# Quarter-array keys and scores, a half-plain first product for batch 1, a snapshot sum on VectorE, and a new written order

## The chip, the cores and the metric

The kernel runs on one core of a Trainium2 chip. The metric is the device time of one execution in microseconds (us). The core has five engines that run side by side and meet at semaphores: TensorE (PE in the profile, with its weight loads as a row of their own, PEld), VectorE (DVE), ScalarE (ACT), GpSimd (POOL) and SyncE (SP). Transfers are issued from the queues of POOL and SP here.

## The reference, cut to what matters

Four batches, 8 heads, 768 tokens, 64 values per head. `P` is an 8x8 matrix per batch and head (five rounds of row and column normalisation of `sort_net`).

```
k_sorted[i] = sum_j P[i, j] k_block[j]        (8 blocks of 96 tokens; v the same)
attn        = softmax(q_block k_sorted_block^T / 8) v_sorted_block
x           = heads side by side, [4, 768, 512]
u           = x + real(fft over tokens of fft over features of x)
un          = (u - mean) / sqrt(var + 1e-6)
out         = u + relu(un @ w_ch1) @ w_ch2    (512 -> 2048 -> 512)
```

So each batch has a stage of attention, a stage of Fourier mixing and a stage of two matrix products, called here the first and the second MLP product.

## The kernel before

**Attention** (`kqt`, `scores`, `av`) takes two heads at a time, a pair. A key step (line 1117) multiplies the loaded keys (128 partitions, six tokens in each) by a mask `bdk` that holds `P` of the head, so that the block sum and the transposition are one product; per pair it is 12 matmuls, in two groups of six, each on 128 rows by 64 columns of the array with 128 moving columns. The queries of batches 0 and 1 are transposed by TensorE (line 1148, 12 per pair); those of batches 2 and 3 by DMA. A score step (line 1176) is eight matmuls on 64 rows by 128 columns, 96 moving columns each, and there are two such steps per pair. ScalarE takes the exponential (line 1185), VectorE or ScalarE subtract one (1198, 1200), and `av` (1215) multiplies by the values.

**Fourier mixing** (`dft1`, `dft2`) is products with tables (lines 1299 to 1394) and sums on VectorE (1259 to 1343, 1403, 1417).

**The MLP.** Batch 0 is plain: `ff1` (line 1539) makes 32 steps of four matmuls with 384 moving columns, a relu out of PSUM follows each (1548 on VectorE, 1551 on ScalarE), and the second product is line 1597. Batches 1 to 3 use a form of matrix multiplication with seven block products in place of eight, over the two token halves and two halves of the weights. In the first product (`ff1_seven`, `pair`) a pair of blocks of 128 hidden features takes 14 matmuls (line 1680) in place of 16; running sums in PSUM are copied out by ScalarE (a snapshot, line 1705), VectorE adds them to another bank (1688) and takes the relu (1699); one of the four results has its relu straight out of PSUM on ScalarE (1722). `SEVEN[b]` says which of the eight pairs of a batch take this form; those ahead of it are plain. It needs sums of weights (`w1_sums`, 1639, two halves of four sums) and of inputs (1668). In the second product (`ff2_chunk`, line 1792) each chunk of 128 tokens takes seven products of eight matmuls (p1 to p7). There ScalarE copies two running sums into one tile of 512 columns (1817), and a DMA with addition issued by POOL (1835) adds that tile to `u`, which VectorE's last add (1812) then reads and adds the product to. The results are stored by SP (1561 to 1570) and, for rows that come out reversed, by POOL (1574).

**What sets the order.** All work is registered as numbered steps (`P.add`), with what each reads and writes. `ORDER` is a written list of step numbers for each engine; `Plan.schedule` replays it with estimated durations to choose the buffers. The numbers count the calls of `P.add`, so adding a step shifts all later ones. `MODE`, `TRIM` and `FETCH` only serve these estimates. Early on, TensorE is fed with idle matmuls (line 1951) until the first Fourier stage of batch 0 is done.

## Time and profile before

| | |
|---|---|
| median of 3 runs | 258.97 us (258.86 to 259.05) |
| the profiled execution | 259.09 us, its span 257.3 us |
| granted TensorE clock, mean | 0.997 |
| busy: PE / PEld / DVE / ACT / POOL | 244.6 / 166.5 / 229.7 / 177.5 / 63.0 us |
| instructions | 6768, of them 2596 matmuls and as many weight loads |

The span is from the first to the last instruction; the 1.8 us beside it are the start and the end of the execution, which the profile does not show. A matmul's row is longer than its turn: a new one starts while the last one drains, so the turn is read from the distance of starts, not from the mean duration. An add that waits for several things is put down to the one that came last.

### The profile page before, as it was taken

How to read it: one execution, taken by the hardware profiler on the slowest of the kernel's cores; microseconds unless marked ns; L12 is line 12 of the kernel's file. 1: busy time of each engine (PE TensorE's matmuls, PEld its weight loads, DVE VectorE, ACT ScalarE, POOL GpSimd, SP SyncE). 2: the span in 40 equal slices, each digit the busy share in tenths (PEclk: the TensorE clock that was granted, in tenths of full speed). 3: DMA queues.
4: the chain of work that ended last, by engine and by line, in shares of the span. 5: the costliest groups of instructions: out<-in, count | busy, mean ns of one | idle time of the engine just before them, and what ended most of it. 6: DMA issues, size and time to landing. Idle time of an engine off the chain costs nothing.

```text
span 257.3 us, 6768 instructions
## 1 busy us (share of the span) xinstructions
PE 244.6 (95%) x2596; PEld 166.5 (65%) x2596; DVE 229.7 (89%) x616; ACT 177.5 (69%) x410; POOL 63.0 (24%) x90
## 2 busy tenths in 40 slices
PE   4799999999999999999999999999999999999990
PEld 1346775576765756655665558887567887568880
DVE  4799999999999999999999999969999976999651
ACT  2599999989879999999828875437985315772110
POOL 8985123323200480000005001322000113001560
PEclk9999999999999999999999999999999999999998
DMA  7999999999980599555605303872221533000496
GB/s 136 201 222 300 221 208 216 206 245 189 166 107 3 95 193 194 132 124 98 199 9 161 132 1 85 176 199 44 82 23 23 102 64 82 3 0 0 103 254 217
DMA packets 46566, 33.53 MB, mean 130 GB/s; under 512 B 30554, under 2 KB 39528, under 8 KB 46532
## 3 DMA queue, kind: packets, MB, share of 16 engines
q0 software_dynamic: 24832, 20.67, 47.5%
q1 hardware_dynamic: 21702, 12.43, 20.8%
q8 instruction: 20, 0.33, 0.5%
q14 instruction: 12, 0.10, 0.2%
HBM read 31.39 MB, written 8.65 MB: 156 GB/s over the span
## 4 chain that ended last, share of the span: by engine, by line
PE 79%; DVE 13%; DMA 3%; ACT 2%; issue 1%; DVEq 0%; ACTq 0%
PE bank L1680 21%; PE bank L1792 20%; PE bank L1597 8%; PE bank L1539 7%; PE bank L1215 4%; PE bank L1176 2%; PE bank L948 2%; DMA u<-vsf 2%; PE bank L1299 2%; PE bank L1390 2%; PE bank L1117 2%; DVE rt L1234 2%; PE bank L1049 1%; PE bank L1394 1%; DVE eb L1198 1%
## 5 line engine op out<-in xcount | busy, mean ns | idle before, releaser
L1705 ACT COPY vsf<-bank 128x384 f32<-128x384 f32 x63 | 28.3, 481 | 12.2 <-PE bank L1680 11.3
L1688 DVE TENSOR_TENSOR hr<-bank,vsf 128x384 f16<-128x384 f32 x63 | 32.7, 549 | 0.9 <-PE bank L1680 0.4
L1680 PE MATMUL bank<-ut,w1sb 128*128 128x384 f16 x144 | 31.6, 326 | 0.0
L1792 PEld LDWEIGHTS <-hr 128*128 128x128 f16 x288 | 28.0, 98 | 5.2 <-issue 0.9
L1185 ACT ACTIVATE ex<-bank 96x384 f32<-96x384 f32 x64 | 29.0, 486 | 1.2 <-PE bank L1176 0.6
L1680 PEld LDWEIGHTS <-w1sb 128*128 128x128 f16 x192 | 18.7, 98 | 11.7 <-issue 0.2
L1817 ACT COPY vsf<-bank 128x256 f32<-128x256 f32 x18 | 6.7, 372 | 26.2 <-PE bank L1792 23.1
L1597 PE MATMUL bank<-w2sb,hr 128*128 128x512 f16 x96 | 24.7, 379 | 0.0
L1539 PE MATMUL bank<-ut,w1sb 128*128 128x384 f16 x128 | 24.7, 327 | 0.0
L1792 PEld LDWEIGHTS <-kq 128*128 128x128 f16 x216 | 21.1, 98 | 2.9
L1574 POOL DMA_INDIRECT out_dram<-u,rows x9 | 9.5, 1050 | 52.8 <-DVE u L1604 41.0
L1680 PEld LDWEIGHTS <-vcx 128*128 128x128 f16 x144 | 14.1, 98 | 9.2
L1812 DVE TENSOR_TENSOR u<-bank,u 128x256 f32<-128x256 f32 (+1 forms) x25 | 11.3, 471 | 8.9 <-PE bank L1792 5.1
L626 POOL DMA_DIRECT2D kq<-in_q_dram x18 | 15.1, 854 | 12.3 <-DMA w2sb<-in_moe_w_ch_dram 5.9
L1215 PEld LDWEIGHTS <-eb 97*128 97x128 f16 x416 | 15.6, 98 | 3.7 <-issue 0.7
L1792 PE MATMUL bank<-w2sb,hr 128*128 128x256 f16 x144 | 17.9, 273 | 0.0
L1792 PE MATMUL bank<-kq 128*128 128x256 f16 x144 | 17.8, 273 | 0.0
L1835 POOL DMA_DIRECT2D u<-vsf x6 | 5.4, 894 | 49.2 <-ACT vsf L1817 49.2
L1200 ACT ACTIVATE eb<-ex,negone 96x384 f16<-96x384 f32 x28 | 17.3, 616 | 0.1
L1215 PE MATMUL bank<-vsf,eb 97*128 97x65 f16 x416 | 17.0, 193 | 0.3 <-DVE vsf L842 0.2
L1234 DVE TENSOR_TENSOR rt<-bank,rz 128x384 f16<-128x384 f32 x32 | 16.9, 545 | 0.2
L1539 PEld LDWEIGHTS <-w1sb 128*128 128x128 f16 x128 | 11.1, 98 | 7.2 <-issue 0.3
(200 smaller groups left out, 593.1 us busy)
## 6 DMA issues: line engine op xcount, KB each, us to landing
kq<-in_k_dram POOLq DMA_DIRECT2D x6, 384.0 KB, 11.9
spilled<-u SPq DMA_DIRECT2D x9, 256.0 KB
u<-spilled SPq DMA_DIRECT2D x9, 256.0 KB, 4.4
w1sb<-in_moe_w_ch_dram POOLq DMA_DIRECT2D x4, 512.0 KB, 19.9
w2sb<-in_moe_w_ch_dram POOLq DMA_DIRECT2D x4, 512.0 KB, 20.3
hr<-in_v_dram POOLq DMA_DIRECT2D x2, 768.0 KB, 9.0
kq<-in_v_dram POOLq DMA_DIRECT2D x2, 768.0 KB, 15.6
kq<-in_q_dram POOLq DMA_DIRECT2D x16, 96.0 KB, 7.2
```

Source lines behind the costliest of these rows:

```text
L626: o = P.add({eng: c}, lambda _: e.dma_start(dst, src), r=r, w=w, prio=prio, nbytes=nbytes, tag="load", after=after)
L1185: nc.scalar.activation(ex.ap[0:96], pss[h2].ap[0:96, 0:384], AF.Exp, scale=SCALE),
L1200: nc.scalar.activation(ed, src, AF.Identity, bias=negone[0:96])
L1215: nc.tensor.matmul(po.ap[:, 65 * T:65 * T + 65], eb.ap[:, e0:e0 + 128], vsf[0:97, vi:vi + 65], start=(n == 0), stop=(n == len(WIN[T]) - 1) ...
L1234: V.tensor_tensor(rt.ap[:, :, D * h:D * h + D], po3()[:, :, 0:D], rz.ap[:, :, None].broadcast_to([128, 6, D]), op=ALU.mult)
L1539: nc.tensor.matmul(ps.ap[:, 0:GT], w1sb[:, c, 128 * fc:128 * fc + 128], ut.ap[:, c, :], start=(c == 0), stop=(c == 3))
L1597: nc.tensor.matmul(ps.ap, hr[g][:, fc, 128 * tt:128 * tt + 128], w2sb[:, fc, :], start=(fc == 0), stop=(fc == 15))
L1680: nc.tensor.matmul(ps.ap[:, 0:GT], lhs[:, c, fi], rhs()[:, c, :], start=(start and c == 0), stop=(c == 1), skip_group_check=True)
L1688: return P.add({"DVE": (0.47, 0.57)}, lambda _: V.tensor_tensor(hr[g][:, fc, :], p.ap[:, 0:GT], flat(o).bitcast(F32), op=ALU.add), r=r, w= ...
L1705: P.add({"ACT": act(GT)}, lambda _: nc.scalar.copy(flat(x).bitcast(F32), A.ap[:, 0:GT]), r=[A], w=[x], prio=pr_v - 1, tag="pc")
L1792: nc.tensor.matmul(ps.ap[:, o:o + 256], lhs()[:, fc], rhs[:, fc], start=(start and fc == 0), stop=(fc == 7), skip_group_check=True)
L1812: P.add({"DVE": (c, c + 0.1)}, lambda _: V.tensor_tensor(u.ap[:, lo:lo + n], p.ap[:, o:o + n], u.ap[:, lo:lo + n], op=ALU.add), r=r, w=w, ...
```

## The change

Five edits:

1. `SEVEN[1]` is (4, 8) in place of (0, 8): the first four of the eight pairs of batch 1 take the plain form of 16 matmuls, with four relus out of PSUM each. The first half of `w1_sums` is then made ahead of batch 2.
2. `QUAD`: for batches 1 to 3 the key step is 24 matmuls on 64 rows by 64 columns with 64 moving columns, four after each other on the four quarters of the array; the two row halves go to two PSUM banks, and one evacuation of 384 columns follows each. The tokens lie otherwise for it: each half of the keys is loaded by two DMAs of 64 partitions, which wait for all earlier users of the place (`gone`). The mask has eight columns per block in place of 16, from a permuted copy of `P` (`make_tk8`: one more matmul, one evacuation and one small load). The score step is 16 matmuls on quarters, still 96 moving columns. The queries of batch 1 are transposed by 24 matmuls on quarters and evacuated in two halves.
3. In the very last chunk VectorE adds the snapshot tile to `u` (`xadd`), in place of the DMA with addition.
4. `FLEX`: the relu of the seven-product form, and a subtraction in the value path, may also stand on ScalarE.
5. All five lists are new. TensorE has 494 steps before and 471 after, ScalarE 398 and 414, VectorE 604 and 570, POOL 74 and 80, SP 79 and 79.

In TensorE's list, the steps of keys, transposes and scores of batches 1 to 3 have these numbers. Before: keys 332, 348, 364, 380 (and each plus 2), 588, 603, 618, 633 (plus 2), 683, 698, 713, 728 (plus 2); transposes 336, 352, 368, 384; scores 338, 354, 370, 386, 593, 608, 623, 638, 688, 703, 718, 733 (and each plus 5). After: keys 337, 353, 369, 385, 595, 609, 623, 637, 688, 702, 716, 730; transposes 340, 356, 372, 388; scores 343, 359, 375, 391, 599, 613, 627, 641, 692, 706, 720, 734 (and each plus 5). The last chunk is, after: p6 1599, xadd 1601, p7 1602 (its add 1603), p4 1604 (1605), p2 1607 (1608, store 1609), p3 1610 (1611, store 1612); 1588, 1585 are p4 and p3 of the chunk before it (add 1586).

```diff
-SEVEN = {0: (8, 8), 1: (0, 8), 2: (0, 8), 3: (0, 8)}
+SEVEN = {0: (8, 8), 1: (4, 8), 2: (0, 8), 3: (0, 8)}
-FLEX = ()
+FLEX = ("relu", "vcd")
 ORDER = { "PE": (
...
-        "205 325 332 348 334 350 352 315 327 321 244 248 250 257 255 338 384 "
-        "259 263 267 343 284 289 430 364 368 366 431 294 275 432 278 281 396 "
-        "354 854 359 1648 380 870 399 564 868 382 860 402 405 386 856 304 571 "
-        "848 850 572 846 852 308 391 370 864 858 375 872 417 414 312 844 411 "
-        "842 408 603 588 605 590 862 449 874 866 497 501 465 886 503 447 875 "
-        "463 876 475 459 877 593 473 887 598 608 618 888 461 445 613 508 889 "
-        "455 510 620 633 457 471 467 469 453 451 512 516 520 880 648 537 881 "
-        "657 542 882 892 623 635 883 651 628 902 912 906 654 894 638 910 908 "
-        "900 643 698 683 918 547 914 896 660 700 685 922 663 904 898 666 916 "
-        "703 669 920 927 688 928 708 693 929 713 728 930 730 715 743 933 777 "
-        "746 934 718 752 749 781 979 978 783 723 733 935 738 788 755 939 764 "
...
-        "1603 1615 1600 1618 1630 1620 1634 1623 1637 1639 1645 1642 "
+        "325 331 356 340 323 329 319 246 250 252 257 259 337 261 265 269 343 "
+        "435 291 296 436 437 277 286 280 283 353 348 865 359 1613 843 853 401 "
+        "369 364 857 404 845 571 873 410 863 407 578 851 306 450 859 579 388 "
+        "385 867 847 372 861 310 871 391 375 855 849 380 396 869 881 464 452 "
+        "882 875 609 595 462 883 416 413 314 422 419 884 468 470 876 478 480 "
+        "877 599 466 903 613 604 878 456 895 476 887 454 637 618 911 460 458 "
+        "888 474 504 623 905 472 901 651 917 654 657 508 889 641 660 890 921 "
+        "627 646 893 515 897 909 517 510 669 899 923 688 632 519 907 523 527 "
+        "913 544 549 663 934 666 716 915 672 935 919 936 720 692 937 928 554 "
+        "725 697 940 929 941 702 730 942 778 744 930 756 931 782 706 759 747 "
+        "784 791 964 734 711 962 952 739 753 789 750 956 762 990 765 954 1007 "
...
+        "1578 1563 1575 1568 1580 1565 1583 1595 1597 1599 1588 1602 1585 "
+        "1604 1610 1607 "
...
     "DVE": (
...
+        "1584 1593 1566 1569 1589 1598 1603 1586 1605 1601 1611 1608 "
...
+QUAD = (1, 2, 3)
...
+        if nm == "k" and b in QUAD:
...
+            for n in range(2):
+                load(qk16(nm, b, hf).rearrange("p h r d -> p h (r d)")[
+                    64 * n:64 * n + 64],
+                    src[b, 4 * hf:4 * hf + 4].rearrange(
+                        "h (w e r) d -> e w h (r d)", e=2, r=6)[n],
+                    393216, keys[2 * n:2 * n + 2], prio, after=after,
+                    gone=gone)
...
+    def make_tk8():
+        load_c("perm", 29.0)
+        pt = Buf("pf")
+        flat = tkh.rearrange("p i b -> p (i b)")
+        P.add(pe(0.12, 1), lambda _: nc.tensor.matmul(
+            pt.ap[:, 0:256], perm[:, 0:128], flat), r=["perm", "tkh"],
+            w=[pt], tag="tk8")
+        P.add(evac(256), lambda e: copy(e, flat, pt.ap[:, 0:256]),
+              r=[pt], w=["tkh"], tag="tk8e")
...
+    def q_four(b, hp):
...
+            for r in range(6):
+                for n in range(2):
+                    for h2 in range(2):
+                        c = slice(64 * n, 64 * n + 64)
+                        nc.tensor.matmul(
+                            pts[n].ap.bitcast(F16)[
+                                64 * h2:64 * h2 + 64, 64 * r:64 * r + 64],
+                            q16[c, 2 * hl + h2, r, :], idh[c, c],
+                            is_transpose=True)
...
+    def kq_four(b, hp, k16, ks):
...
+            for r in range(6):
+                for n in range(2):
+                    for h2 in range(2):
+                        c = slice(64 * n, 64 * n + 64)
+                        nc.tensor.matmul(
+                            pss[n].ap[64 * h2:64 * h2 + 64,
+                                      64 * r:64 * r + 64],
+                            k16[c, 2 * hl + h2, r, :],
+                            bdk8[c, 2 * hp + h2].rearrange("p i c -> p (i c)"))
...
     def scores(b, hp):
...
-                    for h2 in range(2):
-                        rows = slice(64 * h2, 64 * h2 + 64)
-                        nc.tensor.matmul(
-                            pss[h2].ap[:, BLK * j:BLK * j + BLK],
-                            ks.ap[rows, 4 * g + j, :],
-                            qt.ap[rows, c0:c0 + BLK])
+                    for n in range(2 if four else 1):
+                        for h2 in range(2):
+                            c = slice(64 * n, 64 * n + (64 if four else 128))
+                            rows = slice(64 * h2, 64 * h2 + 64)
+                            nc.tensor.matmul(
+                                pss[h2].ap[c, BLK * j:BLK * j + BLK],
+                                ks.ap[rows, 4 * g + j, c],
+                                qt.ap[rows, c0:c0 + BLK])
...
+            if final:
+                P.add({"DVE": (0.6, 0.69)}, lambda _: V.tensor_tensor(
+                    u0.ap, u0.ap, x_(0, 512), op=ALU.add),
+                    r=[(X, 0), (X, 1), u0], w=[(u0, "x")], prio=pr_v,
+                    tag="xadd")
+                return
             P.add({"POOL": (1.0, 4.0)}, lambda _: nc.gpsimd.dma_start(
                 u0.ap, x_(0, 512), accum_op=ALU.add),
                 r=[(X, 0), (X, 1), u0], w=[(u0, "x")], prio=pr_v, tag="xacc")
```

More of the change, by code (lines that the diff above doesn't have):

```diff
@@ L621, with load @@
     w2v = moe_w_ch2.rearrange("(c p) m -> p c m", p=128)
-    def load(dst, src, nbytes, w, prio, eng="POOL", r=(), after=()):
+    def load(dst, src, nbytes, w, prio, eng="POOL", r=(), after=(), gone=()):
         e = {"POOL": nc.gpsimd, "SP": nc.sync}[eng]
@@ L626, in load @@
         o = P.add({eng: c}, lambda _: e.dma_start(dst, src), r=r, w=w,
-                  prio=prio, nbytes=nbytes, tag="load", after=after)
+                  prio=prio, nbytes=nbytes, tag="load",
+                  after=list(after) + list(gone))
         o.late = 6.0 if after else 0.0
@@ L675, in load_qk @@
                     after=after)
+            return
+        if nm == "k" and b in QUAD:
+            keys = kqk(slot[nm, b, hf])
+            gone = set()
+            for x in keys:
+                gone.update(P.wr.get(x, ()))
+                gone.update(P.rd.get(x, ()))
+            for n in range(2):
[5 more added lines that the diff above has]
+                    gone=gone)
             return
```

112 lines of the change are left out of this document (84 added, 28 removed), and 187 rows, old and new, of the table ORDER.

## The prediction

> **What bounds the kernel now.** I read the page's sums first, then the chain that ended last, then the busy time by stage, then single instructions at the end and around the key and score steps.
>
> ```profile
> PE 244.6 (95%) x2596; PEld 166.5 (65%) x2596; DVE 229.7 (89%) x616; ACT 177.5 (69%) x410; POOL 63.0 (24%) x90
> ...
> PE 79%; DVE 13%; DMA 3%; ACT 2%; issue 1%; DVEq 0%; ACTq 0%
> ```
>
> TensorE carries 79% of the chain, VectorE 13%. A mean hides that these lie in different stages. The pieces of the chain (start, length, what):
>
> ```profile
> 49.66 0.91 DVE un L1484 x2
> ...
> 58.53 0.76 PE bank L1539 x4
> ...
> 136.84 15.47 PE bank L1680 x94
> ...
> 155.36 10.48 PE bank L1792 x96
> ...
> 233.00 13.11 PE bank L1792 x120
> 246.13 0.38 ACT vsf L1817
> 246.81 5.89 DMA u<-vsf
> 252.79 0.42 DVE u L1812
> ```
>
> And the busy time by stage (first column the stretch, then PE, PEld, DVE, ACT, POOL, granted clock, DMA share, GB/s):
>
> ```profile
> 33.00:57.00 24.00, 23.72 (x365) 15.88 (x365) 23.45 (x72) 22.43 (x55) 7.20 (x10) 1.00 1.15 216
> 98.00:122.00 24.00, 24.00 (x313) 14.37 (x312) 22.98 (x58) 23.08 (x58) 0.00 (x0) 1.00 0.71 136
> 137.00:170.00 33.00, 33.00 (x248) 23.76 (x246) 30.82 (x90) 22.08 (x53) 5.55 (x8) 1.00 0.49 123
> 246.00:257.30 11.30, 4.62 (x41) 3.74 (x39) 2.60 (x7) 0.37 (x1) 3.46 (x6) 0.92 0.77 239
> ```
>
> Three parts are to be seen. Up to about 58 us the chain is on VectorE, with ScalarE full beside it (23.45 and 22.43 of 24 us). From 58.53 to 246 it is TensorE, without a gap: 94 matmuls of 384 columns in 15.47 us are 0.165 us each, 120 of 256 columns in 13.11 us are 0.109, so 0.43 ns a column, the same in both. Then comes an end of 11 us in which TensorE works for 4.62. There the chain is the accumulating DMA, 5.89 us. So three things pay: less turn time on TensorE after 58 us, less in that end, and less VectorE and ScalarE work ahead of 58 us.
>
> **The end: the snapshot sum on VectorE.** The last instructions in order of time (start, length),
>
> ```profile
> 246.81 1.04 PE L1792 MATMUL bank<-tab,hr 128*128 128x256 f16 x8
> 247.88 0.76 DVE L1812 TENSOR_TENSOR u<-bank,u 128x256 f32<-128x256 f32 x2 [1.21 <-PE bank L1792]
> 248.36 1.03 PE L1792 MATMUL bank<-kq,hr 128*128 128x256 f16 x8 [0.52 <-DVE u L1812]
> 249.23 1.04 PE L1792 MATMUL bank<-w2sb,kq 128*128 128x256 f16 x8
> 250.10 1.04 PE L1792 MATMUL bank<-w2sb,hr 128*128 128x256 f16 x8
> ...
> 250.23 0.96 POOL L1574 DMA_INDIRECT out_dram<-u,rows  x1 [0.19 <-issue]
> 252.79 0.76 DVE L1812 TENSOR_TENSOR u<-bank,u 128x256 f32<-128x256 f32 x2 [2.94 <-DMA u<-vsf]
> 253.24 0.91 SPq L1561 DMA_DIRECT2D out_dram<-u  x2
> ```
>
> and two groups of VectorE (busy us, mean ns):
>
> ```profile
> L1812 DVE TENSOR_TENSOR u<-bank,u 128x512 f32<-128x512 f32 x5 | 3.4, 682 | 0.0
> ...
> L1639 DVE TENSOR_TENSOR vcx<-w1sb 128x1024 f16<-128x1024 f16 x2 | 1.4, 682 | 0.0
> ```
>
> The last product ends at 250.10 + 1.04 = 251.14, but the two last adds wait until 252.79 for the DMA and end at 253.55. Without it, the add of the last product can end at 251.14 + 0.42 = 251.56 and a little: 1.95 us earlier. The store behind it stays as it is (253.55 to the span's 257.3). What the new add costs: nearest row is an add of 512 columns, 0.68. It stands in VectorE's new list behind p4's add (1605) and ahead of those of p3 and p2. From p4's end VectorE then has 0.42 + 0.68 + 0.42 = 1.52 us of work up to its last add; TensorE takes 2 x 0.87 = 1.74 us for p3 and p2, so it is covered. With no cover it would cost 0.68.
>
> **The wait ahead of p4.** Products start 0.87 us apart, but 246.81 to 248.36 is 1.55: p4 waits for the add of p7 (the 0.52 shown). The new list puts a product of the chunk before (1585) between p7 and p4: 0.68 us less. That product's add (1586) still reads what a DMA accumulates, and behind 1586 on VectorE wait 1605, 1601 and all the rest. The DMA starts after product 1580; up to the end of 1585 there are 8 products, 7.0 us, against 0.4 + 5.9 of copy and DMA. The margin is small (0.7 us), and what the DMA is late beyond it comes straight off this gain.
>
> **The first product of batch 1.** Four pairs take 16 matmuls in place of 14: 8 x 0.165 = 1.3 us more on TensorE. On the others:
>
> ```profile
> L1688 DVE TENSOR_TENSOR hr<-bank,vsf 128x384 f16<-128x384 f32 x63 | 32.7, 549 | 0.9 <-PE bank L1680 0.4 <-ACT vsf L1705 0.2
> ...
> L1705 ACT COPY vsf<-bank 128x384 f32<-128x384 f32 x63 | 28.3, 481 | 12.2 <-PE bank L1680 11.3
> ...
> L1699 DVE TENSOR_SCALAR hr<-hr 128x384 f16<-128x384 f16 x72 | 15.6, 248 | 0.0
> ...
> L1551 ACT ACTIVATE hr<-bank 128x384 f16<-128x384 f32 x28 | 13.3, 495 | 1.3 <-PE bank L1539 1.1
> ...
> L842 ACT COPY qt<-bank 128x768 f16<-128x768 f16 x7 | 5.6, 818 | 0.0
> L626 POOL DMA_DIRECT2D kq<-in_k_dram x6 | 4.5, 758 | 25.8 <-DVE eb L1198 21.0 <-DMA w2sb<-in_moe_w_ch_dram 2.8 <-DMA w1sb<-in_moe_w_ch_dram 2.0
> ...
> L826 DVE TENSOR_TENSOR bdk<-tkh,pack 128x1024 f16<-128x1024 f16 x3 | 3.6, 1199 | 0.0
> ```
>
> VectorE loses 12 x 0.549 + 12 x 0.248 = 9.6 us, ScalarE 12 x 0.481 + 4 x 0.495 = 7.8; 16 relus of 0.495 (7.9 us) come back on either. These lie beside a TensorE that has no gap from 136.84 on, so I count them as nothing. The moved half of the weight sums only changes places under the same cover; if that cover is gone it costs its own time, four adds of 0.68 us.
>
> **Keys, transposes, scores on quarters.** Four pieces of TensorE in a row:
>
> ```profile
> 100.80 2.12 PE L1539 MATMUL bank<-ut,w1sb 128*128 128x384 f16 x12
> 102.86 0.34 PE L1176 MATMUL bank<-qt,ks 64*128 64x96 f16 x8
> 103.13 0.53 PE L1117 MATMUL bank<-bdk,kq 128*64 128x128 f16 x12
> 103.59 0.66 PE L1539 MATMUL bank<-ut,w1sb 128*128 128x384 f16 x3
> ```
>
> Starts give the turns. Twelve matmuls of 384 columns are 1.95 us, but the next piece starts after 2.06: 0.1 us is lost where the shape of the array changes. The score step has 0.27 us: eight matmuls run two at a time, 4 x 96 columns are 0.165, and 0.1 is lost again. The key steps have 0.46: six turns of 128 columns are 0.33, and 0.13 is the change and a slow first turn.
>
> Small matmuls and weight loads, by the chain (first row) and by groups (the rest):
>
> ```profile
> 91.66 0.40 PE bank L1215 x13
> ...
> L1304 PEld LDWEIGHTS <-eo 128*1 128x1 f16 x8 | 0.7, 84 | 0.6
> ...
> L1117 PEld LDWEIGHTS <-kq 128*64 128x64 f16 x144 | 4.5, 109 | 2.3 <-issue 1.9
> ...
> L948 PEld LDWEIGHTS <-vcx 128*96 128x96 f16 x4 | 0.5, 124 | 0.0
> ...
> L1215 PEld LDWEIGHTS <-eb 97*128 97x128 f16 x416 | 15.6, 98 | 3.7 <-issue 0.7
> ```
>
> - Keys: 24 matmuls in six turns of four with 64 columns. At 0.43 ns a column a turn is 27 ns, so 0.165 in place of 0.33; bounds per pair are a saving of 0.165 and nothing (the pace of now). I take 31 ns a turn, as the 13 matmuls of 65 columns show it (0.40 / 13): 0.14 x 12 pairs = 1.7 us less.
> - Transposes of batch 1, the same shape: 0.14 x 4 = 0.56 less.
> - Scores: four turns of 96 columns as before, so nothing; if only two quarters run at a time, 0.165 more in each of 24.
> - Changes of shape: keys, transposes and scores now share one shape. Counting in TensorE's lists where a step of these numbers stands next to one of another shape gives 64 changes before and 50 after: 14 x 0.1 = 1.4 us less (1.8 at 0.13).
> - The permuted mask: one matmul of 256 columns, 0.11 more.
>
> Weight loads decide whether a turn can be that short. One column takes 84 ns, 64 take 109, 96 take 124: 0.41 ns for each further column, so 64 columns need some 26 ns of a turn of 27 to 31. It is tight, but it fits. The 128-column load is shorter (98) than the 64-column one, so the score step gives up a faster kind of load. The Trainium skill speaks against the change here: "TensorE: Matmul & The Clock Gate", section "LDWEIGHTS (loading the stationary operand)", gives a load as columns / 1.2 in ns, 53 ns for 64 columns, and "TensorEngine Tiling (Array Packing)", section "Gotcha 2: Feature Incompatibilities", says that column tiling goes without the fast weight load. By that a turn of four would last 53 ns, and the sum would be that of the first rival. This trace's rows differ (0.41 ns a column, not 0.83).
>
> On the other engines: three masks of half the size, at 1.2 each, save VectorE some 1.8 us; eight evacuations of 384 columns (0.49, as the relu of that size) in place of four of 0.82 cost 0.65; one more evacuation under 0.5. Six more key loads cost POOL 6 x 0.76 = 4.6 us of a queue that is busy 24%, and the small load comes ahead of batch 1's keys: these and the query loads behind them start up to 3 x 0.76 = 2.3 us later on POOL. The transfers themselves are full in that time (DMA share 1.15 up to 57 us), so bytes and not issues set them, and I take 0; the bound is 2.3. There are some 390 more matmuls, with as many loads, to be fetched as instructions; of the chain 1% is "issue", and I take 0.
>
> **The order.** In the new list fewer steps of batch 1 stand ahead of the first MLP step (keys 337, 353, scores 343, 348, transposes 340, 356; before, six key groups, four transposes and three scores). So ahead of 58 us VectorE and ScalarE have less to do, and TensorE has it to do later, under full load. I take 0. Either side is bounded by what was moved: at the saved rates above, about 2 us of TensorE turns, and about as much of earlier start.
>
> **The sum.** 259.09 is the profiled execution, 0.12 above the median. TensorE: +1.3 - 1.7 - 0.56 - 1.4 + 0.1 = -2.26. End: -1.95 - 0.68 = -2.63. Together -4.9: 254.2 from 259.09, 254.1 from 258.97; I say 254.2.
>
> **Rivals.**
> 1. The weight loads pace the quarters: a turn of four takes 55 ns, that of the key steps now. Keys and transposes then save nothing, and scores cost 24 x 4 x (55 - 41) ns = 1.3 more. TensorE: +1.3 + 1.3 - 1.4 + 0.1 = +1.3, with the end 259.09 - 1.3 = 257.8. For it: the 64-column load is the slow kind. Against: 0.41 ns a column. 0.15.
> 2. Slower: only two quarters run at a time. Keys and transposes save nothing, scores cost 24 x 0.165 = 4.0: TensorE +4.0, end -2.63, 260.4. It decides once a turn of scores costs over 27 ns more than now (2.63 / 96). Against it: pairs run together now, on row halves and on column halves. 0.07.
> 3. The new order waits: batch 1's mask (336) now stands behind batch 0's first sums, its keys are loaded later, and until 58 us VectorE and ScalarE have no slack; each us by which the first MLP step is late is a us at the end. At 2.3 us (the POOL bound) it gives 256.5, at 4.9 it cancels the gain. 0.13, half of it slower.
> 4. The DMA is no loss: other stores end last. The indirect store (POOL) is issued some 3 us ahead of SP's last ones, so this can take back under 1 us; inside the range.
>
> **How the numbers follow.** The forecast, 252.0 to 256.4, has 0.65. No change to tell is within 0.2% (258.45 to 259.49). Slower: rival 2 and half of rival 3, 0.14; same 0.05; faster 0.81. The low end takes keys at the full rate (-0.3), changes at 0.13 (-0.4) and an earlier start of 1.5: 252.0. The high end reaches over rival 1 to 259.0 and leaves rival 2 and the worse half of 3 outside.
>
> **What would show it.** The last chain without the accumulating DMA, and some 5.2 us from the last product's start to the span's end (now 7.2). No wait ahead of p4. Key groups of 24 with starts within 0.17 to 0.19 us; 0.32 speaks for rival 1 or 2. Score groups of 16 within 0.165; 0.22 for rival 1, 0.33 for 2. TensorE without gaps between 60 and 245. The first MLP step at 55 to 59; at 61 it is rival 3. VectorE's busy sum lower by 8 to 12 us without effect of its own. The prediction is wrong if the key and score groups are longer than now, or if TensorE shows new waits for VectorE or for key loads.

## The result, and the profile after

The new kernel takes 256.39 us (median of 4 executions, 255.73 to 256.75) against 258.92 us (258.80 to 259.05) for the old one beside it: a ratio of 0.9892 with a 95% interval of 0.9877 to 0.9908. It is 2.5 us faster, where 4.8 were forecast. The profiled execution took 256.75 us with a span of 255.0 us, so it is 0.36 us above the median.

The profile of the new kernel, its sums by engine and the chain by engine:

```profile
PE 244.4 (96%) x2992; PEld 166.9 (65%) x2992; DVE 224.0 (88%) x582; ACT 183.5 (72%) x426; POOL 65.8 (26%) x96
...
PE 91%; DMA 3%; ACT 2%; issue 1%; DVE 1%; DVEq 0%; POOLq 0%
```

TensorE's share of the chain rises from 79% to 91% (85% in a second profiled execution of the same kernel, after_again below, so some points of it are scatter), yet its busy time stays where it was (244.6, now 244.4). The chain's pieces behind the first MLP step, and its last five:

```profile
137.95 2.60 PE bank L1646 x16
140.77 1.95 PE bank L1646 x12
...
217.33 14.95 PE bank L1787 x92
232.28 18.35 PE bank L1899 x168
250.63 0.02 issue
250.66 0.42 DVE u L1919
251.08 0.33 DVEq L2092
```

The accumulating DMA is gone from the chain: 168 products of 256 columns run without a break up to the last adds. The timeline of the new kernel's end (start, length, what, and idle time before it):

```profile
246.09 1.04 PE L1899 MATMUL bank<-tab,hr 128*128 128x256 f16 x8
...
246.96 1.04 PE L1899 MATMUL bank<-w2sb,kq 128*128 128x256 f16 x8
...
247.84 1.04 PE L1899 MATMUL bank<-kq,hr 128*128 128x256 f16 x8
...
248.71 1.04 PE L1899 MATMUL bank<-w2sb,kq 128*128 128x256 f16 x8
248.76 0.36 SPq L1671 DMA_DIRECT2D out_dram<-u  x1
248.91 0.42 DVE L1919 TENSOR_TENSOR u<-bank,u 128x256 f32<-128x256 f32 x1 [0.18 <-PE bank L1899]
249.25 0.68 DVE L1943 TENSOR_TENSOR u<-u,vsf 128x512 f32<-128x512 f32 x1
249.58 1.04 PE L1899 MATMUL bank<-w2sb,hr 128*128 128x256 f16 x8
...
250.66 0.76 DVE L1919 TENSOR_TENSOR u<-bank,u 128x256 f32<-128x256 f32 x2 [0.72 <-PE bank L1899]
251.11 0.85 SPq L1668 DMA_DIRECT2D out_dram<-u  x2
```

Products start every 0.87 us, the one ahead of p4 too. The new add of 512 columns takes 0.68 us beside the products at 248.71 and 249.58, and the last two adds wait for TensorE alone (0.72).

Now the quarters. The first fence is the new kernel, the second the run after_oldshape further down (the new order with the old shapes), at the same place:

```profile
86.52 0.38 PE L1187 MATMUL bank<-bdk,kq 64*64 64x64 f16 x24
86.73 0.34 PE L1283 MATMUL bank<-qt,ks 64*64 64x96 f16 x16
87.00 0.82 PE L1646 MATMUL bank<-ut,w1sb 128*128 128x384 f16 x4
```

```profile
86.99 0.53 PE L1183 MATMUL bank<-bdk,kq 128*64 128x128 f16 x12
87.45 0.34 PE L1279 MATMUL bank<-qt,ks 64*128 64x96 f16 x8
87.72 0.82 PE L1642 MATMUL bank<-ut,w1sb 128*128 128x384 f16 x4
```

From start to start the key step takes 0.21 us in place of 0.46: half its turns, and no change of shape ahead of the scores. The score step takes 0.27 in both. So the quarters do what was forecast.

Where the gain went shows when TensorE's time is added up by step on both sides of the first MLP product. The time of a step is its columns at 0.417 ns each, halved or quartered where two or four run side by side (products of 384 columns follow each other every 162 ns); what a start is later than that is put down to a change of shape (up to 0.097 us each), to small gaps (under 40 ns) or to longer ones.

| us of TensorE | ahead: before | after | oldshape | behind: before | after | oldshape |
|---|---|---|---|---|---|---|
| keys | 2.24 | 1.60 | 1.92 | 2.88 | 1.60 | 3.20 |
| transposes of queries | 2.56 | 1.60 | 1.92 | 0 | 0.32 | 0.64 |
| scores and value products | 4.93 | 4.42 | 4.42 | 11.46 | 11.97 | 11.97 |
| first MLP product | - | - | - | 74.24 | 75.52 | 75.52 |
| changes of shape | 4.35 | 4.17 | 4.26 | 5.81 | 4.83 | 4.94 |
| idle matmuls | 6.60 | 7.20 | 7.20 | - | - | - |
| small gaps | 1.15 | 1.28 | 1.11 | 4.76 | 5.02 | 4.46 |
| longer gaps | 5.98 | 7.03 | 6.36 | 1.58 | 1.30 | 1.07 |
| first MLP product starts at | 52.76 | 52.42 | 52.16 | | | |
| last matmul starts at | | | | 250.87 | 250.35 | 251.33 |

Steps that did not change are left out. Three differences make the profiled gain of 2.3 us of span. The first MLP product starts 0.34 us earlier. The stretch from there to the last matmul is 0.18 us shorter (198.11 to 197.93): keys -1.28, changes -0.98, longer gaps -0.28, but the plain pairs +1.28, steps moved behind the first MLP product +0.83 (transposes 0.32, scores and value products 0.51) and small gaps +0.26. And the end, from the last matmul's start to the end of the span, is 1.80 us shorter (6.42 to 4.63). Ahead of the first MLP product 2.1 us of keys, transposes and moved steps are gone from TensorE, and 1.65 of them came back as longer gaps (+1.05) and idle matmuls (+0.6). These are two executions; in after_again the first MLP product starts 0.26 us earlier still (52.16), the stretch behind it is 197.49 us and the end 4.64, so tenths in the first two differences are scatter, and the end is not.

### The profile page after: what moved, and what is told of

Same layout as the page of the kernel before. It is cut to its first block, busy times and chain, and to the rows that moved or that the text cites. A ratio compares the mean times of both kernels' runs of the same rounds, so it can differ in the third digit from the quotient of the medians.

```text
span 255.0 us, 7548 instructions
## 1 busy us (share of the span) xinstructions
PE 244.4 (96%) x2992; PEld 166.9 (65%) x2992; DVE 224.0 (88%) x582; ACT 183.5 (72%) x426; POOL 65.8 (26%) x96
## 4 chain that ended last, share of the span: by engine, by line
PE 91%; DMA 3%; ACT 2%; issue 1%; DVE 1%; DVEq 0%; POOLq 0%
PE bank L1899 22%; PE bank L1787 18%; PE bank L1646 13%; PE bank L1704 8%; PE bank L1322 5%; PE bank L993 3%; DMA hr<-in_v_dram 3%; PE bank L1283 3%; PE bank L1497 3%; PE bank L1406 3%; PE bank L2064 2%; PE bank L905 2%; PE bank L999 1%; PE bank L1501 1%; PE bank L1187 1%; PE bank L1094 1%
## 5 line engine op out<-in xcount | busy, mean ns | idle before, releaser
L1646 PE MATMUL bank<-ut,w1sb 128*128 128x384 f16 x192 | 37.2, 326 | 0.0
L1795 DVE TENSOR_TENSOR hr<-bank,vsf 128x384 f16<-128x384 f32 x56 | 29.3, 552 | 4.2 <-PE bank L1787 2.7
L1812 ACT COPY vsf<-bank 128x384 f32<-128x384 f32 x56 | 25.4, 482 | 9.4 <-PE bank L1787 8.9
L1292 ACT ACTIVATE ex<-bank 96x384 f32<-96x384 f32 x64 | 28.0, 486 | 4.9 <-PE bank L1283 2.8
L1787 PE MATMUL bank<-ut,w1sb 128*128 128x384 f16 x120 | 25.7, 326 | 0.0
L1704 PE MATMUL bank<-w2sb,hr 128*128 128x512 f16 x96 | 24.0, 379 | 0.0
L1646 PEld LDWEIGHTS <-w1sb 128*128 128x128 f16 x192 | 17.0, 98 | 10.4 <-issue 0.2
L1658 ACT ACTIVATE hr<-bank 128x384 f16<-128x384 f32 x42 | 20.0, 491 | 3.5 <-PE bank L1646 3.2
L1787 PEld LDWEIGHTS <-w1sb 128*128 128x128 f16 x160 | 15.6, 98 | 9.2
L1787 PEld LDWEIGHTS <-vcx 128*128 128x128 f16 x120 | 11.7, 98 | 7.5
L1948 POOL DMA_DIRECT2D u<-vsf x5 | 4.5, 910 | 46.4 <-ACT vsf L1924 46.4
```

What stands on the lines that cost most here:

```text
L1292: nc.scalar.activation(ex.ap[0:96], pss[h2].ap[0:96, 0:384], AF.Exp, scale=SCALE),
L1646: nc.tensor.matmul(ps.ap[:, 0:GT], w1sb[:, c, 128 * fc:128 * fc + 128], ut.ap[:, c, :], start=(c == 0), stop=(c == 3))
L1658: nc.scalar.activation(hr[g][:, fc, :], ps.ap[:, 0:GT], AF.Relu)
L1704: nc.tensor.matmul(ps.ap, hr[g][:, fc, 128 * tt:128 * tt + 128], w2sb[:, fc, :], start=(fc == 0), stop=(fc == 15))
L1787: nc.tensor.matmul(ps.ap[:, 0:GT], lhs[:, c, fi], rhs()[:, c, :], start=(start and c == 0), stop=(c == 1), skip_group_check=True)
L1795: return P.add({"DVE": (0.47, 0.57)}, lambda _: V.tensor_tensor(hr[g][:, fc, :], p.ap[:, 0:GT], flat(o).bitcast(F32), op=ALU.add), r=r, w= ...
```

## The experiments

They were timed in four groups. Beside them the kernel before took 258.89, 258.92, 258.81 and 258.78 us (medians; all its executions lay within 258.59 and 259.42). The new kernel itself was timed beside the first group alone (256.18), and in the first measurement (256.39); where a later run is compared with it, both are named as a span.

### Which parts make the gain at the end

The new kernel as it is, for comparison:

> The changed kernel as it is, as the control for the runs beside it. Both theories: 256.4 us, between 255.7 and 256.8.

Measured: 256.18 us (255.67 to 256.79), ratio 0.9898 (0.9883 to 0.9913). The kernel repeats, with a scatter of 1.1 us as in the first measurement (1.0, where the old one had 0.25; here that had 0.8).

The old kernel with the new sum alone:

```diff
             snap(1)
+            if final:
+                P.add({"DVE": (0.6, 0.69)}, lambda _: V.tensor_tensor(
+                    u0.ap, u0.ap, x_(0, 512), op=ALU.add),
+                    r=[(X, 0), (X, 1), u0], w=[(u0, "x")], prio=pr_v,
+                    tag="xadd")
+                return
-        "1605 1636 1625 1641 "          (POOL)
+        "1605 1625 1641 "
-        "1624 1640 1646 1643 "          (DVE)
+        "1624 1640 1636 1646 1643 "
```

> The kernel before with one edit: the last snapshot sum on VectorE (right behind p4's add) in place of the accumulating DMA. Theory 1 (TensorE's savings count only behind the first MLP steps; the end gives its full price): 258.9 - 1.95 = 257.0. Theory 2 (the end is hidden anyway, the measured gain of the change is TensorE's): within 0.5 of 258.9.

Measured: 257.69 us (257.51 to 258.01), ratio 0.9955 (0.9942 to 0.9969): 1.2 us less, not 1.95. The timeline of its end:

```profile
249.29 0.42 DVE L1812 TENSOR_TENSOR u<-bank,u 128x256 f32<-128x256 f32 x1 [0.79 <-PE bank L1792]
249.59 0.38 SPq L1564 DMA_DIRECT2D out_dram<-u  x1
249.63 0.68 DVE L1836 TENSOR_TENSOR u<-u,vsf 128x512 f32<-128x512 f32 x1
251.04 0.76 DVE L1812 TENSOR_TENSOR u<-bank,u 128x256 f32<-128x256 f32 x2 [0.72 <-PE bank L1792]
251.49 0.83 SPq L1561 DMA_DIRECT2D out_dram<-u  x2
```

The last add ends at 251.80, 1.75 us earlier than before; but from there to the end of the span (256.2) it is 4.4 us in place of 3.75. So 0.65 us was given back behind the add. The store ahead of the last ones is now issued 1.9 us before them, in place of 3.55 (249.69 to 253.24 in the old kernel); that this is why the last ones take longer was not tried.

The new kernel with the accumulating DMA put back:

```diff
-            if final:
+            if False:
                 P.add({"DVE": (0.6, 0.69)}, lambda _: V.tensor_tensor(
-        "1584 1593 1566 1569 1589 1598 1603 1586 1605 1601 1611 1608 "   (DVE)
+        "1584 1593 1566 1569 1589 1598 1603 1586 1605 1611 1608 "
-        "1406 1366 1386 1562 1582 1570 1590 1606 "                       (POOL)
+        "1406 1366 1386 1562 1582 1570 1601 1590 1606 "
```

> The changed kernel with one edit undone: the last snapshot sum by the accumulating DMA again. Theory 1: 256.4 + 1.95 = 258.4, so that the rest of the change is worth some 0.5 us. Theory 2: within 0.5 of 256.4.

Measured: 256.39 us (255.73 to 256.59), ratio 0.9902 (0.9889 to 0.9916): no difference to the new kernel. The timeline of its end:

```profile
244.96 0.90 POOL L1948 DMA_DIRECT2D u<-vsf  x1
...
247.78 0.42 DVE L1919 TENSOR_TENSOR u<-bank,u 128x256 f32<-128x256 f32 x1 [0.18 <-PE bank L1899]
...
249.53 0.76 DVE L1919 TENSOR_TENSOR u<-bank,u 128x256 f32<-128x256 f32 x2 [1.32 <-PE bank L1899]
249.98 0.85 SPq L1668 DMA_DIRECT2D out_dram<-u  x2
```

The last adds wait for TensorE (1.32), not for the DMA: it is issued at 244.96 and lands 3.36 us later, at 248.32, with 1.2 us to spare. In the old kernel it was issued at 246.81 and landed 5.89 us later. The room for it is nearly the same in both: from its issue to the end of the last product there are 4.3 us in the old order (to 251.14) and 4.5 in this run (to 249.49). So it isn't that more products cover the DMA; it lands sooner. The queue of SP's stores, between the DMA's issue and its landing (packets, MB, share of the 16 engines), first in the old kernel and then in this run:

```profile
q1 hardware_dynamic: 565, 0.96, 52.5%
```

```profile
q1 hardware_dynamic: 30, 0.02, 2.0%
```

In the old order SP's stores, most of them of the chunk before the last, move 0.96 MB beside the DMA; in the new order those stores are nearly done by then. That these stores are what slows it is likely, but no run changed them alone. From the last matmul's start to the end of the span the old kernel takes 6.42 us, the old order with the sum on VectorE 5.43, the new order with the DMA 4.47, and the new kernel, with both, 4.63. The new order gives the whole gain at the end by itself, the sum alone 1.0 of 1.8, and together they give no more.

### Whether the steps alone would do it

The old order with quarters and the VectorE sum, all eight pairs of the first product with seven products as before, each old step taken over one for one. Its edit is the new kernel's functions under the old lists and the old `SEVEN`, with no other change:

```diff
-SEVEN = {0: (8, 8), 1: (4, 8), 2: (0, 8), 3: (0, 8)}
+SEVEN = {0: (8, 8), 1: (0, 8), 2: (0, 8), 3: (0, 8)}
...
 ORDER = {
-    "PE": ( ... the new list ... )
+    "PE": ( ... the old list, each number replaced by that of the same step ... )
     ... the same for DVE, ACT, POOL and SP ...
```

> The written order of the kernel before, step by step, with the quarters for keys, transposes and scores and the snapshot sum on VectorE, and all eight pairs of batch 1 in the seven-product form. Theory 1: behind the first MLP step stand eight of the twelve pairs' keys and no transposes, 8 x 0.14 = 1.1, some 0.3 for fewer changes of shape, 1.95 at the end: 255.5. If TensorE's savings counted everywhere: 12 x 0.14 + 4 x 0.14 + 0.4 + 1.95 = 4.6, 254.3. If the new order is what is worth something: slower than the changed kernel, above 256.8.

Measured: 265.47 us (265.04 to 266.03), ratio 1.0258 (1.0244 to 1.0272): 6.6 us slower than the old kernel and 9 us slower than the new one. The waits of TensorE in this run (in total, times, longest), the largest behind the loads of the first microseconds:

```profile
PE bank L1190 <- ACT ex L1295: 1.5, 2, 0.8
PE bank L1500 <- ACT ex L1295: 1.0, 1, 1.0
PE bank L1325 <- DVE u L1513: 0.8, 1, 0.8
```

Line 1190 is the key step. In quarters it writes two PSUM banks at once, where the old step wrote one after the other, and in the old order the second bank is still held by scores that ScalarE has not yet evacuated. TensorE's longer gaps between 58 and 120 us, counted as in the table above, add up to 7.8 us. By stage, this run's first MLP product starts 1.97 us later than in the old kernel (54.73), the stretch from there to the last matmul is 5.5 us longer (203.64), and the end is 1.1 us shorter (5.30). So the steps alone are no gain without new lists. The shown waits for the second bank are 1.5 us of the 9; how much more of it they cause, and how much is the order's other differences, this run doesn't separate.

### What a microsecond of TensorE is worth, early and late

```diff
+                if 20.0 < o.start < 46.0 and o.costs["PE"][0] > 0.01:
+                    step += 1
+                    if step % EVERY == 0 and more > 0:      # EVERY = 5, more = 10
+                        more -= 1
+                        nc.tensor.matmul(spin.ap[:, 0:480], idh,
+                                         pack[:, 0:240].bitcast(F16))
```

> The changed kernel (256.3 us) with ten more idle matmuls of 480 columns, 0.2 us each, between steps of TensorE planned from 20 to 46 us, ahead of the first MLP step. Theory 1 (that stretch is not paced by TensorE, so what TensorE saves there is lost): up to 0.7 more, 256.3 to 257.0. Rival 1 (TensorE paces it too, the gain was lost elsewhere): 2.0 more, 258.3.

Measured: 257.61 us (257.46 to 257.81), ratio 0.9946 (0.9932 to 0.9959): 1.2 to 1.4 us of the 2.0 arrive at the end, between the two expectations. (The last part of this section shows what took the rest.)

```diff
-                for c in range(4):
+                for c in ((0, 1, 2, 2, 3) if (b, g) == (0, 1) and fc < 12
+                          else range(4)):
                     nc.tensor.matmul(ps.ap[:, 0:GT], w1sb[...], ut.ap[:, c, :], ...)
```

> The changed kernel with twelve more matmuls of 384 columns in batch 0's first MLP product, behind the first MLP step (one block product is added twice there, so that product differs). Both theories: 12 x 0.165 = 2.0 more, 258.3. If VectorE and ScalarE, full in that stretch, pace it in truth: under 0.7 more.

Measured: 258.07 us (257.58 to 258.48), ratio 0.9962 (0.9949 to 0.9976): 1.7 to 1.9 us of 1.95. In that product nearly all of TensorE's time counts.

The counterpart takes the changed shapes away and keeps the order:

```diff
-                for n in range(2):
-                    for h2 in range(2):
-                        c = slice(64 * n, 64 * n + 64)
-                        nc.tensor.matmul(pss[n].ap[64 * h2:64 * h2 + 64, 64 * r:64 * r + 64],
-                            k16[c, 2 * hl + h2, r, :], bdk8[c, 2 * hp + h2]...)
+                for h2 in range(2):
+                    nc.tensor.matmul(pss[r // 3].ap[64 * h2:64 * h2 + 64,
+                                                    128 * (r % 3):128 * (r % 3) + 128],
+                        k16[:, 2 * hl + h2, r, :], bdk[:, 2 * hp + h2]...)
     (the transposes likewise, and the scores with one matmul of 128 columns for two of 64)
```

> The new order with the keys' matmuls and the queries' transposes in their old shapes, in place (same steps, buffers and waits; only the columns' places in the key and query tiles are the old ones, so the values of batches 1 to 3 are wrong). By the sums of TensorE's time in the trace this adds 1.3 us of keys and 0.1 to 0.3 of transposes behind the first MLP step, and 0.64 of keys and 0.3 to 0.5 of transposes ahead of it. Theory A (behind it all counts, ahead of it 0.65 of it): +2.0 to +2.4, so 258.2 to 258.8. Rival 1 (what is ahead of it is given back to waits entirely): +1.4 to +1.6, 257.6 to 258.0. Rival 2 (all counts, and the changes of array shape that go away are priced in full too): +2.6 to +3.2, 258.9 to 259.6.

Measured: 257.51 us (257.15 to 258.17), ratio 0.9947 (0.9935 to 0.9959): 1.1 to 1.3 us more than the new kernel. The table above has its column. Behind the first MLP product keys and transposes take 1.92 us more, and small gaps and longer ones 0.8 less, 1.24 together, changes included; ahead of it they take 0.64 more, and the first MLP product starts at 52.16, no later than in the new kernel. This is nearest to rival 1 of that expectation, and a little less: what the quarters save early returned nothing here, and the quarters as a whole are worth 1.2 us in the new kernel. That the early part returned nothing has to do with a load, as the last part of this section shows.

### What holds the early stretch

Four runs ask why. First VectorE's subtractions of batch 0:

```diff
-                        ap=[ee_[0:96, :].ap[0], [224, 4], [1, BLK]])
+                        ap=[ee_[0:96, :].ap[0], [224, 4], [1, NQ]])   # NQ = 8 in batch 0
-                        "p (j q) -> p j q", q=BLK)
+                        "p (j q) -> p j q", q=BLK)[:, :, 0:NQ]
```

> The changed kernel with batch 0's 16 subtractions of one on 8 of 96 columns each (the rest of its attention weights is left out). That takes some 0.25 us from each on VectorE and 0.35 on ScalarE, about 4.5 us of both together, all ahead of the first MLP step. Theory 1a (VectorE and ScalarE pace that stretch): 1.0 to 2.2 less, 254.1 to 255.3. Theory 1b (loads or the chain of single steps pace it): within 0.4 of 256.3.

Measured: 256.06 us (255.97 to 256.16), ratio 0.9886 (0.9871 to 0.9901). Then the exponentials too (the same slice on both operands of the activation):

> The new kernel with batch 0's 16 exponentials and 16 subtractions on 8 of every 96 columns (the other columns of those tiles are left out, so batch 0's weights are wrong): some 16 x 0.28 us less on ScalarE and 16 x 0.15 less of subtraction, nothing changed on TensorE. Theory A (the early stretch is held by ScalarE's list: the chain of waits runs through its evacuations and exponentials from 28 to 31 us, and TensorE waits 0.7 us for a value evacuation at 25 us): the first MLP product starts 0.6 to 1.3 us earlier and the kernel takes 255.0 to 255.7. Theory B (it is held by loads, or by single steps in a row, not by ScalarE's amount of work): within 0.3 us of the new kernel, 255.9 to 256.5, as with the subtractions alone.

Measured: 255.89 us (255.50 to 256.49), ratio 0.9892 (0.9878 to 0.9907), first MLP product at 51.59. Both medians lie in the lower half of the new kernel's own scatter. Leaving that work of VectorE and ScalarE out brought 0.5 us at most, and the next part finds another cause for that much.

Next the new layout of the keys. The new evacuation writes every second fp16 element of a row, the old one runs of them; this run writes runs:

```diff
-                e, ks.ap.rearrange("p i (r c e) -> p e r i c", e=2, c=8)[
+                e, ks.ap.rearrange("p i (e r c) -> p e r i c", e=2, c=8)[
                     :, half, 0:6],
```

> The changed kernel with the keys' evacuation writing runs of eight next to each other in place of every second element (the order of a block's keys then no longer fits that of its values). The evacuation took 590 ns on ScalarE after the change and 486 before, 22 times: 2.3 us of ScalarE. Theory 1: the larger part lies beside a TensorE that is full, 0 to 0.5 less, 255.8 to 256.3. Rival 2 (the slower evacuation is what ate TensorE's gain): 1 to 2 less, 254.3 to 255.3.

The groups of ScalarE's key evacuations (busy us, mean ns of one), of the new kernel and of this run:

```profile
L887 ACT CAST ks<-bank 128x384 f16<-128x384 f32 x22 | 12.0, 592 | 0.8 <-PE bank L1187 0.7
```

```profile
L887 ACT CAST ks<-bank 128x384 f16<-128x384 f32 x22 | 9.8, 479 | 0.8 <-PE bank L1187 0.7
```

Measured: 256.63 us (256.42 to 256.68), ratio 0.9907 (0.9891 to 0.9922). The layout costs ScalarE 2.2 us, and the kernel nothing: without that cost it is no faster, and a little above the range of theory 1 (255.8 to 256.3).

Then the idle matmuls themselves, the last 14 of 36 left out:

```diff
                     for _ in range(spins(t, o.start - 0.05)):
+                        left -= 1            # left = 22
+                        if left < 0:
+                            break
                         nc.tensor.matmul(
```

> The new kernel without the last 14 of its 36 idle matmuls (nine stand at 15 to 20 us, three at 30 to 35, two near 42); 14 x 0.2 = 2.8 us of TensorE less. Theory A (an early microsecond of TensorE costs 0.65 us wherever it stands, as the ten added idle matmuls cost 1.3 of their 2.0): 1.8 us less than the new kernel's 256.2 to 256.4, so about 254.5. Theory B (the idle matmuls stand where TensorE's next step has no input yet, and only fill gaps): no change, 256.0 to 256.5, with the granted clock still near 1.00. Rival C (without them the granted clock falls): over 256.8 with a clock under 0.99.

Measured: 255.82 us (255.50 to 257.42, 6 executions), ratio 0.9894 (0.9873 to 0.9914), first MLP product at 51.76, granted clock of the profiled execution 1.000. The waits of TensorE between 12 and 53 us in this run:

```profile
PE bank L1252 <- DMA kq<-in_q_dram: 1.4, 1, 1.4
PE bank L1161 <- issue: 0.5, 1, 0.5
PE bank L1283 <- ACT qt L887: 0.4, 1, 0.4
```

Where the idle matmuls stood there are now waits: 2.8 us of them went, and the longer gaps grew from 7.03 to 10.31. They had filled gaps. The largest of these is a load: the queries land at 16.3 us, in this run, in the new kernel and in the old (16.5), so what TensorE saves ahead of that moment can't bring their transposes forward.

### A second load, and the scatter

A comparison of the runs so far shows one more wait of the new order. The timeline of the run after_again (the new kernel):

```profile
25.71 1.35 PEld L1094 LDWEIGHTS bank<-tab,un 128*64 128x64 f32 x16 [0.80 <-ACT vsf L887]
25.74 1.45 PE L1094 MATMUL bank<-tab,un 128*64 128x129 f32 x15 [0.52 <-DMA tab<-k_tab]
```

TensorE waits for the f32 table of batch 0's sine and cosine products. From the transfers and the lists:

| run | table lands | line 1094 starts | first MLP product |
|---|---|---|---|
| after | 25.86 | 25.99 | 52.42 |
| keys_dense | 25.67 | 25.8 | 52.53 |
| after_again | 25.60 | 25.74 | 52.16 |
| after_dma | 25.16 | 25.3 | 51.72 |
| late_waste | 25.16 | 25.3 | 51.72 |
| early_cut | 24.84 | 25.3 | 51.73 |
| exp_cut | 25.04 | 25.2 | 51.59 |
| after_oldshape | 25.54 | 25.7 | 52.16 |

Where the table is late, the products start 0.13 us behind it (in the row of the run after the wait is put down to ScalarE, whose evacuation ended at the same moment), and the first MLP product moves with it. In the old order the table landed at 24.79 and was read at 25.6. The test swaps two loads on POOL:

```diff
-        "20 21 22 23 7 8 9 3 4 5 6 12 10 24 25 26 27 28 29 333 119 120 121 "
+        "20 21 22 23 7 8 9 3 4 5 6 12 10 24 25 26 27 29 28 333 119 120 121 "
```

> The new kernel with one pair of loads swapped on POOL's queue: the f32 table (0.53 MB) that the sine and cosine products of batch 0 read is issued ahead of the table cs (0.59 MB), which is first read at 40 us. In the new order those products come up at 25.2 us, and the table, issued at 14.6 to 14.8, lands 10.1 to 11.2 us later: the profiles of the new kernel and its variants show TensorE held there for 0.77, 0.59, 0.28 or 0 us, and the first MLP product starts at 52.42, 52.16, 51.72 and 51.6 to 51.7 with it. Theory A (this load sets most of the new kernel's scatter of 1 us from run to run, and costs its median half of it): the table lands near 23 us, no wait ahead of line 1094, the first MLP product at 51.6 to 51.8, median 255.6 to 255.9 and nearly all executions within 0.5 us. Theory B (the early stretch gives that back at its next waits, on ScalarE's and VectorE's steps): no wait there, but the median 256.1 to 256.4 and the scatter as before.

Measured: 255.73 us (255.51 to 255.88), ratio 0.9878 (0.9860 to 0.9895), first MLP product at 51.70. The table's rows in this run:

```profile
L1094 PE MATMUL bank<-tab,un x16: 271/273/324, 25.1 to 26.5; 128*64 128x129 f32 x8, 128*64 128x128 f32 x8
L629 POOL DMA_DIRECT2D tab<-k_tab x1: 562/562/562, 15.0 to 15.0; - x1
...
DMA to landing us min/median/max: 7.6/7.6/7.6
```

It lands at 22.56, nobody waits for it, and the first MLP product starts 1.06 us earlier than in the old kernel, where the new one had gained 0.34 and 0.60. This is theory A: the load cost the median 0.45 to 0.66 us (255.73 against 256.18 and 256.39; the intervals of the ratios still overlap, and the two weren't timed side by side). The four executions lie within 0.4 us; that the whole scatter of the new kernel was this load's is less firm, since one of the six executions of fewer_spins, whose profile has no wait for it, took 257.42. That one had a granted clock of 0.993 where the other five had 1.000; the old kernel ran at 0.992 to 0.998 without such a difference, so the clock alone is not shown to be the reason. The version is the fastest of the study, 3.05 us below the old kernel.

With this the earlier runs read differently. The subtractions and exponentials were cut in kernels whose profiled executions had an early table (24.84 and 25.04), so their 0.1 to 0.5 us need no other cause. And of the ten idle matmuls of early_waste two stand ahead of line 1094, which starts at 26.0 there, after the table (25.43): the wait of 0.6 to 0.8 us is gone, and with it that much of the 2.0. Against table_first, which has no such wait either, the ten cost nearly all of their time: the first MLP product starts 1.85 us later, and the kernel takes 1.9 us more (1.7 by the differences to the old kernel beside each).

In after_oldshape the wait is 0.24 in place of 0.59 (after_again), so the old shapes' extra time ahead of line 1094 vanished in it: in both runs that line starts some 0.13 us behind the table, at 25.67 and 25.74. Without the wait it could have started at about 25.43 in after_oldshape, against 25.14 in table_first. So some 0.3 of the 0.64 us would have counted with an early table; this is an estimate from two traces, no run tried it.

## Why the prediction was right or wrong, step by step

The direction held, and so did the shorter turns and the fewer changes of shape. The size was half of what was forecast, because of two steps: what is saved on TensorE early was counted in full, and the end's gain was given to the wrong part. That 256.39 lies within 252.0 to 256.4 is luck: it is 0.01 us inside, and single executions lie on both sides of the end. The wider end of 259.0 that the text names held with room.

- **Plain pairs, +1.3.** The trace has +1.28 behind the first MLP product (0.16 for each of eight products; the 0.165 of the forecast, and its 0.43 ns a column, divide a piece of the chain that ends with the drain of its last product). No run undid this part alone; the late matmuls of the same size cost 1.7 to 1.9 of 1.95.
- **Keys, -1.7, and transposes, -0.56.** The turns came out as forecast (24 key matmuls from first to last start in 0.190 us, 16 score matmuls in 0.161), and rivals 1 and 2 fall. An estimate by the rule that the Trainium skill gives in "TensorE: Matmul & The Clock Gate", section "LDWEIGHTS (loading the stationary operand)", would be six turns of 53 ns, 0.32 us; the trace disagrees. What failed is the step from TensorE's time to the kernel's: I counted all twelve key groups and the transposes as if they lay on a TensorE without a gap. Of the keys' saving only 1.28 us lies there, and of the transposes none: the two of four that moved behind the first MLP product add 0.32. The rest stands ahead of it, where after_oldshape shows that it returned nothing. My own first view said that the chain of the early stretch lies on VectorE, and the sum took no account of it. The runs don't bear that view out either: leaving out VectorE's and ScalarE's work there brought 0.5 us at most, and added TensorE time counts there (early_waste). Part of the saving was held by the load of a table (table_first); for the rest the cause stays open.
- **Changes of shape, -1.4.** 1.16 by the trace, 0.98 of it behind the first MLP product. Against it stand 0.3 us (against the old kernel) to 0.6 us (against after_oldshape) of small gaps that I had not counted; a part of them is that a turn of the new key step takes 32 ns, where its columns alone would take 27.
- **The mask, +0.1.** 0.11, early.
- **The end, -1.95 for the VectorE sum.** The end became 1.80 us shorter, but I gave it to the wrong part: after_dma keeps the DMA and is as fast, since in the new order the DMA lands after 3.36 us, where I had taken the 5.89 of the old order as given. In the old order the sum brings 1.2, and the stores drain 0.65 us more slowly. I had written that the store behind it stays as it is; my rival 4 had this at under 1 us.
- **The wait ahead of p4, -0.68.** It is gone, as forecast; the longer gaps behind the first MLP product fall by 0.3 to 0.8 altogether in the two profiled executions of the new kernel.
- **The order, 0.** This is the second step that failed. The moved steps cost 0.83 us behind the first MLP product (the 0.32 of transposes among them), and the lighter stretch ahead of it brought its start forward by 0.34 to 0.60 only; with the table's load out of the way it is 1.06. I had bounded it from both sides by 2 us, which holds. Rival 3 named the place and the kind (loads on POOL, an early stretch without slack) but the wrong load: not the keys of batch 1, but a table that TensorE had not waited for in the old order.
- **Evacuations of the keys, taken as the same 0.49.** They take 0.59. It cost nothing, as keys_dense shows.
- **VectorE's busy time, 8 to 12 us lower.** It fell by 5.7 (229.7 to 224.0), and ScalarE's rose by 6.0 (177.5 to 183.5). Neither shows in the time: behind the first MLP product TensorE waited for VectorE once in the old kernel (0.5, ahead of p4) and waits for no other engine in the new one.
- **The first MLP step at 55 to 59.** It started at 52.4. I had taken the first piece of the chain on that line (58.53) for the first step, which in the old kernel starts at 52.76.

In sum, for the two profiled executions: 4.9 forecast, 2.3 found. Of the missing 2.6 us, 0.42 are keys, 0.88 transposes, 0.42 changes and 0.15 the end; the other moved steps add 0.51, the small gaps 0.26, and the longer gaps behind the first MLP product fell by 0.28 and not 0.68 (0.40). The earlier start gave 0.34 back, and the mask (0.1) lies where it doesn't count.

What stays open: with the table early (table_first), 1.06 of the 2.1 us saved ahead of the first MLP product come back; the other half lies in gaps of 0.1 to 0.4 us (behind changes to the value products and ahead of the second score step) that no run took apart. The idle matmuls that were left out became waits for the queries and for ScalarE, so these gaps have more than one cause. Old_order_quads was not taken apart, the plain pairs were not undone alone, and the stores beside the DMA were not moved alone.

## What to carry to other kernels

Before a saving on the busiest engine is counted, split it at the moments that loads or other engines fix: of 0.64 us saved in the stretch with such a moment nothing came back here, and of a microsecond added behind it 0.9 counted. When an order is searched anew, look in the new trace for inputs that were never waited for before; one such load cost some 0.5 us here, and moving it one place up its queue gave that back. And try a gain in the other order as well: two parts that each remove the same wait can't be added, as the sum on VectorE and the new order of the end show.

## What the runs showed of the hardware that was not expected

- Four quarters of 64 rows and 64 columns ran at 32 ns a turn of 64 moving columns, each turn with four weight loads of its own; the first turn of a step took 53. A change between array shapes cost up to some 0.1 us, in both kernels.
- An evacuation of 128x384 from f32 to fp16 on ScalarE took 592 ns where it wrote every second element and 479 where it wrote runs of eight.
- The accumulating DMA that took 5.89 us at the end of the old kernel landed within 3.36 us in after_dma, where SP's stores moved 0.02 MB beside it in place of 0.96. That the stores are the reason was not tried.
- Leaving out 14 of the 36 idle matmuls left the granted clock at 1.000 over the span in five of six executions (0.993 in the sixth).
